# Float64 weights to float32: the sign written over the low word in place, in a 16-bit operation

## The chip, the cores and the metric

The kernel runs on one core of one Trainium2 chip. The metric is the device time of one execution in microseconds (us). The kernel before takes 461.08 us, the median of 3 runs (460.72 to 461.09). A few tenths of a microsecond is therefore what one run differs from the next.

## The reference

The reference is a recurrent attention (a gated outer-product state) followed by a multiplicative feed-forward block:

```python
f = 1 / (1 + exp(-f_logit))                       # B=4, H=8, S=768, D=48
for t in range(S):
    state = f[:, :, t, :, None] * state + einsum('bhd,bhe->bhde', k[:, :, t], v[:, :, t])
    y[:, :, t] = einsum('bhd,bhde->bhe', q[:, :, t], state)
x = y.transpose(0, 2, 1, 3).reshape(3072, 384)
a, b = x @ w1, x @ w2                             # 384 -> 1024
out = ((a * b) @ w3) @ w_out                      # 1024 -> 1024 -> 384
```

q, k, v and f_logit are float32. The four weight matrices are **float64**, because they are drawn as such and never cast. The chip's engines here work in float32, so the kernel reads every weight as a pair of 32-bit words and makes a float32 from them itself. That conversion is what the change touches.

## The kernel before, in words

**Stages.** The sequence is cut into 24 chunks of 128 positions (`NU`), which the kernel calls u = 0 to 23. For each chunk VectorE makes two scans of the gates (L529, L551) and scales q and k with them (L545 gives Q, L559 gives K), TensorE makes the pair products and the values (L582, L656, L675, L689, and L596 turns K), ScalarE copies, GpSimd masks (L712). Four chunks make a block of 512 tokens, and there are six blocks for the feed-forward part. Block 0 uses plain products (`up`, which calls the helper of L901), the later ones use schemes with fewer multiplications (L997, L1152). w3 and w_out are multiplied with each other once on the chip, in eight "folds" of eight matrix products (L1470), so that the block's second and third product become one.

**The conversion** is `fetch`. A piece of a weight matrix is loaded by DMA into a staging area of the tile `place` as pairs of 32-bit words, low word first. Four operations then make float32 of it:

1. `rest` on ScalarE (L1406) reads the low word as an integer and writes the float 2 + low * 2^-51 over it, so the low word's bits are 0x40000000 plus a small rounding carry. In its upper half there is always 0x4000.
2. `shifted` on VectorE (L1421) writes the high word, shifted left by 3, into the scratch `magnitudes`.
3. `signed` on VectorE (L1425) takes the sign bit of the high word, ors it with the low word from step 1, and writes the result to the destination (`dst()`).
4. `joined` on VectorE (L1431) adds the scratch to the destination as 32-bit integers. In the profile this integer addition is a custom operation that reads and writes 16-bit halves, so 1024 words are 2048 elements.

There are 16 pieces: A, C, B and D (the halves of w1 and w2, 1536 words per partition each), four of w_out (768 words) and eight of w3 (1024 words). A piece of w_out or w3 goes into one of three staging places, in turn, so that a load must wait until the piece that was there is no longer read. `got` names the operation after which the place is free.

**What sets the order.** The program is written as tasks with an engine, a cost, dependencies and a priority (`Plan`). A list scheduler plays them through with those costs and writes each engine's instructions in the order it found. Each engine then works strictly in this order and waits on semaphores. Where the scheduler finds TensorE without work in the first 130 us (`FULL`), it puts in idle matrix products on a constant tile (L402) to fill the gap:

```python
if t["eng"] == "PE" and t["at"] < FULL:
    n = int((t["at"] - ready_at) / 0.43)
    if ready_at and n:
        idle(n)
```

So a change of one cost can move instructions of every engine, and can put in or leave out idle products. In the trace one matrix product of float32 is two instructions.

Of the kernel before, what the change touches and what calls it, by code (L numbers as in the profile page):

```python
# [37 lines left out]
I32 = mybir.dt.int32  # L38
U32 = mybir.dt.uint32
U16 = mybir.dt.uint16  # L40
ALU = mybir.AluOpType
# [254 lines left out]
def ranged(ctx, tc, q, k, f_logit, v, w1, w2, w3, w_out, out, ident, w12, wc, left):  # L296

    nc = tc.nc
# [38 lines left out]
    def at(a, *shape):  # L337
        n = 1
        for m in shape:
            n *= m  # L340
        t = place[:, a : a + n]
        return t.rearrange("p (a b) -> p a b", a=shape[0]) if len(shape) == 2 else t
# [26 lines left out]
    plan = Plan()  # L369
# [97 lines left out]
    def moves(n, size, rate, emit, deps, prio, late=0.0, since=0.0, lanes=("lane",)):  # L467


        for j in range(n):  # L470
            i = plan.add("SP", 0.45, (lambda: None) if j else emit, [d] if j else deps, prio - j * 1e-3, takes=lanes, lag=0.85, since=since)
            d = i
            t = plan.add("DMA", size / n / rate, lambda: None, [i], prio - j * 1e-3, lag=1.1 + late, frees=[i])
        return t
# [905 lines left out]
    def holders(where, n):  # L1380

        return [g for a, m, gs in users if a < where + n and where < a + m for g in gs]

    def fetch(loads_, where, prio, due, dst, waits=(), deps=()):

        total = sum(n for _, n, _ in loads_)
        if not wide:
            def plain():
                d = dst()
                for at_, n, src in loads_:  # L1390
                    nc.sync.dma_start(d[:, at_ : at_ + n].rearrange("p (a m) -> p a m", a=src.shape[1]), src)
            return [plan.add("SP", 1.9 * total / 512, plain, list(waits), prio, lag=2.0)]
        raw = at(where, 2 * total).bitcast(U32)
        pairs_ = raw.rearrange("p (n two) -> p n two", two=2)
        lo, hi = pairs_[:, :, 0], pairs_[:, :, 1]
        held = holders(where, 2 * total)
        got = []
        users.append((where, 2 * total, got))
        landed, low = [], []
        for i, (at_, n, src) in enumerate(loads_):  # L1400
            def load(at_=at_, n=n, src=src):
                nc.sync.dma_start(raw[:, 2 * at_ : 2 * (at_ + n)].rearrange("p (a m) -> p a m", a=src.shape[1]), src.bitcast(U32))

            def rest(at_=at_, n=n):
                part_ = lo[:, at_ : at_ + n]
                nc.scalar.activation(part_.bitcast(F32), part_, AF.Copy, bias=2.0, scale=2.0**-51)  # L1406

            landed.append(moves(1, n, 400, load, held + list(deps), prio + 0.02 * i, SURE, lanes=("lane", "heavy")))
            asked.append(landed[-1])
            low.append(plan.add("ACT", 0.2 + 0.43 * n / 512, rest, [landed[-1]], due + 0.02 * i))  # L1410
        w = total / 512
        a0 = spot[0] if total <= 512 else (spot[0] + 512) // 1024 * 1024 % 2048
        if a0 + total > 2048:
            a0 = 0
        spot[0] = (a0 + (total + 511) // 512 * 512) % 2048
        m = magnitudes[:, a0 : a0 + total]
        mine = range(a0 // 512, (a0 + total + 511) // 512)
        s = {}

        def shifted():  # L1420
            nc.vector.tensor_scalar(m.bitcast(U32), hi, 3, None, ALU.logical_shift_left)  # L1421

        def signed():
            s["to"] = dst()
            nc.vector.scalar_tensor_tensor(  # L1425
                s["to"].bitcast(U32), hi, 0x80000000, lo, ALU.bitwise_and, ALU.bitwise_or
            )

        def joined():
            to = s["to"].bitcast(I32)  # L1430
            nc.vector.tensor_tensor(to, m.bitcast(I32), to, ALU.add)  # L1431

        past = [joins[i] for i in mine if i in joins]
        h = plan.add("DVE", 0.16 + 0.27 * w, shifted, landed + past, due, shared=True)
        g = plan.add("DVE", 0.16 + 0.53 * w, signed, [*low, h] + list(waits), due)
        j = plan.add("DVE", 0.16 + 0.53 * w, joined, [h, g], due - 1, shared=True)
        parts.append((g, j))
        joins.update({i: j for i in mine})
        got.append(g)
        return [j]  # L1440

    def weights():
        due = dict(zip(((0, 0), (1, 0), (0, 1), (1, 1)), DUE))
        for item in (x for x in EARLY if x in "ABCD"):
            half, which = divmod("ABCD".index(item), 2)
            w = (w1, w2)[which]
            cols = slice(half * KH * P, (half + 1) * KH * P)
            pieces[which, half] = fetch(
                [(kc * KH * P, KH * P, w[kc * P : kc * P + P, cols].unsqueeze(1)) for kc in range(KM)],
                EARLY_AT[item], turn_of(item), due[which, half],  # L1450
                lambda which=which, half=half: w12[:, which, half].rearrange("p k c -> p (k c)"),
            )

    def folding():
        done = []
        for i in range(0, KF, 2):
            src = w_out[i * P : (i + 2) * P].rearrange("(kc p) c -> p kc c", p=P)
            done += fetch(
                [(0, 2 * DM, src)], 2048 * ((13 + i // 2) % NRAW), 25 + 2.2 * i, 45 + 2.2 * i,
                lambda i=i: wos[:, i : i + 2].rearrange("p a c -> p (a c)"),  # L1460
                holders(10240, KF * DM) + [tk[3][nm] for nm in "qvs"], [tk[3]["z"]] if BEHIND and i < BEHIND else [],
            )
# [23 lines left out]
        for jc in range(KF):  # L1486
            src = w3[jc].unsqueeze(1)
            got = fetch(
                [(0, KF * P, src)], 2048 * ((17 + jc) % NRAW), 36 + 6 * jc, 50 + 6 * jc, w3_piece(jc),
                fp[jc - 2 : jc - 1] if jc >= 2 else holders(8192, 2048),  # L1490
            )
            fp.append(plan.add("PE", 5.15, fold(jc), got + done + fp[-1:], 0, takes=["f"]))
            folds.append(plan.add("ACT", 0.48, folded(jc), fp[-1:], -10, frees=fp[-1:]))
# [139 lines left out]
    for t in plan.order():  # L1633
        if t["eng"] == "PE" and t["at"] < FULL:
            n = int((t["at"] - ready_at) / 0.43)
# [382 lines left out]
```

## Time and profile before

| what | value |
|---|---|
| median of the runs | 461.08 us |
| span of the profiled execution, first to last instruction (the page gives no other time of it) | 459.2 us |
| TensorE busy (matrix products) | 450.8 us, 98% |
| VectorE busy | 370.7 us, 81% |
| ScalarE busy | 211.7 us, 46% |
| GpSimd busy | 66.3 us, 14% |
| conversion on VectorE: L1421, L1425, L1431, 16 each | 11.5, 20.5 and 20.9 us |
| conversion on ScalarE: L1406, 24 | 21.2 us |
| granted TensorE clock | 1.00 throughout |

The runs' median lies 1.9 us above the span of the profiled execution. A line of a timeline reads: start, duration, engine, source line, operation, output from inputs, shapes, how many; what follows in brackets is the time that the engine sat idle before it, and what ended that. A line of a group reads: busy time in all, mean ns of one, then the idle time before them with its releasers. "PE" is TensorE, "DVE" VectorE, "ACT" ScalarE, "POOL" GpSimd, "SPq" the queue of SyncE, which issues the DMAs.

### The profile page before, as it was taken

Reading aid. Unit: us, or ns where it says so; the run is one execution under the profiler, and the core shown is the slowest. Engines: PE = TensorE matmul, PEld = TensorE weight load, DVE = VectorE, ACT = ScalarE, POOL = GpSimd, SP = SyncE. Lnnn points to the kernel's source line nnn. Section 1 sums busy time; section 2 is a strip of 40 time slices with the busy share of each in tenths; the row PEclk is TensorE's granted clock in tenths of the full one; section 3 lists DMA queues with packets and bytes.
Section 4 is the critical chain, followed back from the end, with each engine's and each line's share of the span. In section 5 each row is a group of like instructions: output and inputs, shape, how many; then the busy total and the mean of one; then the engine's idle time right before and its main releaser. Section 6 shows DMA issues by size and latency. Waiting matters only on the chain.

```text
span 459.2 us, 11789 instructions
## 1 busy us (share of the span) xinstructions
PE 450.8 (98%) x4792; PEld 394.6 (86%) x4792; DVE 370.7 (81%) x651; ACT 211.7 (46%) x473; POOL 66.3 (14%) x90
## 2 busy tenths in 40 slices
PE   7999999999999999999999999999999999999996
PEld 6788886666899888889999888899899988889996
DVE  8997899999898999989999699896659466767641
ACT  3565344332233453543322256665665666665300
POOL 9331000121222531132222000000000000000000
PEclk9999999999999999999999999999999999999999
DMA  6997898833236664356322602436365522333111
GB/s 180 283 314 239 299 334 299 264 110 104 71 90 196 198 192 128 105 158 177 98 76 63 164 0 93 137 119 211 132 199 177 192 72 93 92 93 91 36 68 40
DMA packets 43309, 68.75 MB, mean 150 GB/s; under 512 B 5217, under 2 KB 28386, under 8 KB 42226
## 3 DMA queue, kind: packets, MB, share of 16 engines
q1 hardware_dynamic: 43250, 67.95, 48.2%
q8 instruction: 39, 0.64, 0.6%
q14 instruction: 20, 0.16, 0.1%
HBM read 58.88 MB, written 9.04 MB: 148 GB/s over the span
## 4 chain that ended last, share of the span: by engine, by line
PE 95%; DVE 1%; SPq 1%; DMA 1%; issue 0%; POOL 0%; POOLq 0%; DVEq 0%
PE f L901 24%; PE l L1152 15%; PE f L997 13%; PE f L1152 12%; PE f L1470 9%; PE l L901 9%; PE py L656 3%; PE pa L582 2%; PE pa L689 2%; PE f L596 2%; PE py L675 2%; PE f L402 1%; SPq L495 1%; DMA ab<-in_k_dram 1%; DVE K L559 0%
## 5 line engine op out<-in xcount | busy, mean ns | idle before, releaser
L712 POOL TENSOR_SCALAR_AFFINE_SELECT A<-A 64x512 f32<-64x512 f32 (+1 forms) x46 | 43.9, 955 | 110.5 <-ACT A L706 108.3
L1470 PE MATMUL f<-place 128*128 128x384 f32 x128 | 42.4, 487 | 0.0
L901 PE MATMUL f<-xt,w 128*128 128x256 f32 x192 | 42.1, 380 | 0.0
L901 PEld LDWEIGHTS f<-xt,w 128*128 128x128 f32 x192 | 36.3, 190 | 5.0
L1470 PEld LDWEIGHTS f<-place 128*128 128x128 f32 x128 | 23.9, 190 | 15.5
L901 PE MATMUL f<-place 128*128 128x192 f32 x176 | 31.9, 327 | 0.0
L997 PE MATMUL f<-xt,w 128*128 128x256 f32 x120 | 31.3, 380 | 0.0
L529 DVE TENSOR_TENSOR_SCAN fwd<-gate,floor 112x512 f32<-112x512 f32 x24 | 30.0, 1251 | 1.3 <-ACT gate L521 0.3
L551 DVE TENSOR_TENSOR_SCAN bwd<-gate,back 112x512 f32<-112x512 f32 x24 | 30.4, 1267 | 0.7
L901 PEld LDWEIGHTS f<-place 128*128 128x128 f32 x176 | 28.9, 190 | 0.4 <-issue 0.2
L848 ACT ACTIVATE ys<-py 112x512 f32<-112x512 f32 x22 | 13.1, 596 | 33.3 <-PE py L675 31.5
L997 PEld LDWEIGHTS f<-xt,w 128*128 128x128 f32 x120 | 22.5, 190 | 2.9
L901 PE MATMUL f<-wc,ab 128*128 128x192 f32 x128 | 23.6, 328 | 0.0
L1406 ACT ACTIVATE place<-place 128x512 f32<-128x512 uint32 (+2 forms) x24 | 21.2, 885 | 4.6 <-DMA place<-in_w_dram 4.0
L812 POOL TENSOR_TENSOR G<-lasts,gate 112x4 f32<-112x4 f32 x20 | 11.7, 586 | 75.1 <-ACT lasts L534 30.4
L901 PEld LDWEIGHTS f<-wc,ab 128*128 128x128 f32 x128 | 21.2, 190 | 0.3
L521 ACT ACTIVATE gate<-f 112x512 f32<-112x512 f32 x22 | 13.9, 632 | 16.0 <-DMA f<-in_f_logit_dram 7.0
L901 PE MATMUL l<-place 128*128 128x192 f32 x112 | 19.8, 326 | 0.0
L656 PEld LDWEIGHTS py<-A,vt 64*64 64x64 f32 (+1 forms) x672 | 13.3, 127 | 7.3 <-issue 6.5
L997 PE MATMUL f<-place 128*128 128x256 f32 x72 | 19.1, 386 | 0.0
L901 PEld LDWEIGHTS l<-place 128*128 128x128 f32 x112 | 18.5, 190 | 0.1
L656 PE MATMUL py<-A,vt 64*64 64x64 f32 (+1 forms) x672 | 18.0, 223 | 0.2
(288 smaller groups left out, 1066.7 us busy)
## 6 DMA issues: line engine op xcount, KB each, us to landing
place<-in_w_dram SPq DMA_DIRECT2D x21, 512.0 KB, 5.4
A<-in_w_dram SPq DMA_DIRECT2D x19, 512.0 KB, 4.0
place<-in_w_dram SPq DMA_DIRECT2D x8, 1024.0 KB, 6.2
q<-in_q_dram SPq DMA_DIRECT2D x46, 96.0 KB, 2.7
vt<-in_v_dram SPq DMA_DIRECT2D x23, 192.0 KB, 3.2
out_dram<-o SPq DMA_DIRECT2D x23, 192.0 KB, 2.9
k<-in_k_dram SPq DMA_DIRECT2D x44, 96.0 KB, 2.4
yt<-ys SPq DMA_DIRECT2D x44, 96.0 KB, 2.7
```

The source lines that it names most:

```text
L521: nc.scalar.activation(gate[u % 2][:, 0:NQ], fu, AF.Sigmoid)
L529: nc.vector.tensor_tensor_scan(s["P"], gate[u % 2][:, 0:NQ], floor, 0.0, ALU.mult, ALU.max)
L551: nc.vector.tensor_tensor_scan(s["R"][:, ::-1], gate[u % 2][:, NQ:0:-1], back[:, ::-1], 0.0, ALU.mult, ALU.max)
L656: done = nc.tensor.matmul(y_block(u, hp, par, half)[p0 : p0 + w], lhsT=s["v"][half * W : half * W + W, h * D : h * D + w], rhs=s["A"][half ...
L712: nc.gpsimd.affine_select(out=a, in_=a, pattern=pattern, compare_op=ALU.is_ge, fill=0.0, base=0, channel_multiplier=-1,)
L812: nc.gpsimd.tensor_tensor(s["G"], lasts[:, u], heads(gate[(u + 1) % 2][:, 0:NQ])[:, :, 0], ALU.mult)
L848: nc.scalar.activation(ys, py, AF.Copy, accum_out=ysum[:, u : u + 1])
L901: nc.tensor.matmul(out_, lhsT=lhs[i], rhs=rhs[i], start=start and i == 0, stop=i == len(lhs) - 1, skip_group_check=True,)
L997: nc.tensor.matmul(q[nm][:, which * TH : which * TH + TH], lhsT=lhs[i](which), rhs=rhs[i], start=start and which == 0 and i == 0, stop=i = ...
L1152: nc.tensor.matmul(banks[g, c][:, which * TH : which * TH + TH], lhsT=lhs, rhs=x_node(a), start=first and which == 0, stop=True, skip_grou ...
L1406: nc.scalar.activation(part_.bitcast(F32), part_, AF.Copy, bias=2.0, scale=2.0**-51)
L1470: nc.tensor.matmul(w3s["p", jc], lhsT=w3s[jc][:, kc * P : kc * P + P], rhs=wos[:, kc], start=(kc == 0), stop=(kc == KF - 1),)
```

## The change

`signed` no longer writes the destination. It works on 16-bit halves in the staging area: it reads the upper half of the high word, keeps the sign bit, ors 0x4000 to it and writes this over the upper half of the low word, which held 0x4000. It has one source instead of two. `joined` then reads the low word where it lies, in the staging area with a step of 8 bytes, adds the scratch, and writes the destination. Three things go with it: the planner's cost for `signed` is 0.16 + 0.27 us per 512 words in place of 0.16 + 0.53; the wait for a free destination moves from `signed` to `joined`; and the staging place is free after `joined` and not after `signed`.

```diff
+        halves_ = raw.bitcast(U16).rearrange("p (n four) -> p n four", four=4)
...
         def signed():
-            s["to"] = dst()
-            nc.vector.scalar_tensor_tensor(
-                s["to"].bitcast(U32), hi, 0x80000000, lo, ALU.bitwise_and, ALU.bitwise_or
-            )
+            nc.vector.tensor_scalar(halves_[:, :, 1], halves_[:, :, 3], 0x8000, 0x4000, ALU.bitwise_and, ALU.bitwise_or)
 
         def joined():
-            to = s["to"].bitcast(I32)
-            nc.vector.tensor_tensor(to, m.bitcast(I32), to, ALU.add)
+            nc.vector.tensor_tensor(dst().bitcast(I32), m.bitcast(I32), lo.bitcast(I32), ALU.add)
...
-        g = plan.add("DVE", 0.16 + 0.53 * w, signed, [*low, h] + list(waits), due)
-        j = plan.add("DVE", 0.16 + 0.53 * w, joined, [h, g], due - 1, shared=True)
+        g = plan.add("DVE", 0.16 + 0.27 * w, signed, [*low, h], due)
+        j = plan.add("DVE", 0.16 + 0.53 * w, joined, [h, g] + list(waits), due - 1, shared=True)
...
-        got.append(g)
+        got.append(j)
```

The lines of the three operations are L1421, L1425 and L1431 before, and L1422, L1425 and L1428 in the changed kernel.

The scheduler writes other orders from the new costs and dependencies. TensorE, where the first feed-forward product of block 0 begins (L901; L689 are the last products of the attention's chunk before it), before:

```order
L689 MATMUL pa<-place,kt 48x48
L402 MATMUL f_507<-floor 128x256 x2
L901 MATMUL f_510<-xt,w_59 128x256 x3
L901 MATMUL f_521<-xt,w_59 128x256 x3
L901 MATMUL f_530<-xt,w_59 128x256 x3
L656 MATMUL py<-A,place 64x64 x2
```

and in the changed kernel:

```order
L689 MATMUL pa<-place,kt 48x48
L901 MATMUL f_505<-xt,w_59 128x256 x3
L901 MATMUL f_515<-xt,w_59 128x256 x3
L901 MATMUL f_525<-xt,w_59 128x256 x3
L656 MATMUL py<-A,place 64x64 x2
```

One batch of idle products is gone. The other batches of L402 stay; the last of them comes further down the order.

VectorE, from the piece D of w2 to the second piece of w_out (shapes of 1536 are D, of 768 w_out; L943 ends a product of block 0), before:

```order
L1431 ISA w_59<-place,w_59 128x3072
L943 TENSOR_TENSOR ab<-f_642,ab 128x256
L529 SCALAR_TENSOR_TENSOR fwd<-gate_95,floor 112x512
L943 TENSOR_TENSOR ab<-f_653,ab 128x256
L1421 TENSOR_SCALAR place<-place 128x768
L1425 SCALAR_TENSOR_TENSOR place<-place 128x768
L1421 TENSOR_SCALAR place<-place 128x768
L943 TENSOR_TENSOR ab<-f_669,ab 128x256
L1425 SCALAR_TENSOR_TENSOR place<-place 128x768
L1431 ISA place<-place 128x1536
```

and in the changed kernel:

```order
L1428 ISA w_59<-place 128x3072
L943 TENSOR_TENSOR ab<-f_638,ab 128x256
L1422 TENSOR_SCALAR place<-place 128x768
L529 SCALAR_TENSOR_TENSOR fwd<-gate_95,floor 112x512
L943 TENSOR_TENSOR ab<-f_648,ab 128x256
L1425 TENSOR_SCALAR place<-place 128x768
L1428 ISA place<-place 128x1536
L943 TENSOR_TENSOR ab<-f_664,ab 128x256
L539 RECIPROCAL back<-fwd 112x4
L551 SCALAR_TENSOR_TENSOR bwd<-gate_95,back 112x512
L1422 TENSOR_SCALAR place<-place 128x768
L943 TENSOR_TENSOR ab<-f_680,ab 128x256
```

The backward scan of chunk 4 (L539, L551) now comes between the first two pieces of w_out; before, it came after all four of them and after two pieces of w3. Its product K (L559) follows it there, and on TensorE the turn of that K (L596) comes ahead of the first fold instead of behind the second.

SyncE, around the load of the fourth piece of w_out (128x2x768; the loads of 128x2048 are w3, L1402 before is L1403 in the changed kernel), before:

```order
L1402 DMA place<-in_w_dram 128x2048
L495 DMA f_103<-in_f_logit_dram 48x512 x2
L1402 DMA place<-in_w_out_dram 128x2x768
L495 DMA k_101<-in_k_dram 48x512 x2
L495 DMA q_99<-in_q_dram 48x512 x2
L1402 DMA place<-in_w_dram 128x2048 x3
```

and in the changed kernel:

```order
L1403 DMA place<-in_w_dram 128x2048
L495 DMA f_103<-in_f_logit_dram 48x512 x2
L495 DMA k_101<-in_k_dram 48x512 x2
L495 DMA q_99<-in_q_dram 48x512 x2
L1403 DMA place<-in_w_out_dram 128x2x768
L1403 DMA place<-in_w_dram 128x2048 x3
```

The load of the fourth piece of w_out now stands behind four loads of chunk 5's k and q.

## The prediction

> **What bounds the kernel now.** I read first the page's busy times and its chain of work that ended last, then the waits of TensorE alone.
>
> ```profile
> PE 450.8 (98%) x4792; PEld 394.6 (86%) x4792; DVE 370.7 (81%) x651; ACT 211.7 (46%) x473; POOL 66.3 (14%) x90
> PE 95%; DVE 1%; SPq 1%; DMA 1%; issue 0%; POOL 0%; POOLq 0%; DVEq 0%
> PE f L402 <- DVE floor L425: 1.7, 1, 1.7
> PE py L596 <- DVE K L559: 0.7, 1, 0.7
> PE pa L689 <- issue: 0.6, 1, 0.6
> PE f L596 <- DVE K L559: 0.4, 1, 0.4
> ```
>
> TensorE is busy for 450.8 of 459.2 us and 95% of the chain is on it. Its waits add up to 3.4 us, and none of them is at a product of the feed-forward part or at a fold (L901, L997, L1152, L1470). So a microsecond less of VectorE work is worth nothing by itself. The time moves only if TensorE gets something out of its way, or has to wait anew. One thing that is in its way isn't counted as a wait: the idle products of L402. Second view, TensorE in order of time where the feed-forward part begins, with the two operations on VectorE that it needs there:
>
> ```profile
> 28.61 0.27 PE L689 MATMUL pa<-place,kt 64*48 64x48 f32 x3
> 29.47 0.67 PE L689 MATMUL pa<-place,kt 64*48 64x48 f32 x29 [0.59 <-issue]
> 30.06 1.13 PE L402 MATMUL f<-floor 112*128 112x256 f32 x4
> 31.03 4.05 PE L901 MATMUL f<-xt,w 128*128 128x256 f32 x18
> 36.39 32.64 PE L901 MATMUL f<-xt,w 128*128 128x256 f32 x150
> 25.91 1.75 DVE L1425 SCALAR_TENSOR_TENSOR w<-place 128x1536 uint32<-128x1536 uint32 x1
> 27.69 1.76 DVE L1431 CUSTOM_DVE_ANT_0 w<-place,w 128x3072 uint16<-128x3072 uint16 x1
> 33.31 2.09 DVE L1431 CUSTOM_DVE_ANT_0 w<-place,w 128x3072 uint16<-128x3072 uint16 x1
> ```
>
> From 30.06 to 31.03 TensorE multiplies a constant. The piece that it needs, A, was ready at 27.69 + 1.76 = 29.45, so here the idle products themselves hold up the work, by 0.97 us. Third view, the busy time of the engines while the weights are converted and folded:
>
> ```profile
> 30.00:50.00 20.00, 19.90 (x154) 17.17 (x151) 15.98 (x17) 9.17 (x21) 4.03 (x3) 1.00 0.86 280
> 50.00:70.00 20.00, 20.00 (x93) 17.33 (x92) 18.03 (x29) 9.05 (x15) 0.20 (x1) 1.00 0.91 315
> 70.00:90.00 20.00, 20.00 (x129) 12.20 (x129) 18.34 (x24) 8.88 (x14) 1.96 (x2) 1.00 0.85 274
> 90.00:110.00 20.00, 20.00 (x296) 13.19 (x295) 19.05 (x25) 7.19 (x16) 4.59 (x6) 1.00 0.45 130
> ```
>
> The columns after the stretch's length are PE, PEld, DVE, ACT and POOL. VectorE has 4.02 + 1.97 = 5.99 us idle between 30 and 70, and 1.66 + 0.95 = 2.61 between 70 and 110. It is nearly as full as TensorE, and that idle time is all that it could take on without TensorE noticing.
>
> **The change part by part.** The prices come from the groups of the three operations, by shape:
>
> ```profile
> L1421 DVE TENSOR_SCALAR place<-place 128x1024 uint32<-128x1024 uint32 x8 | 5.5, 704 | 0.0
> L1421 DVE TENSOR_SCALAR place<-place 128x1536 uint32<-128x1536 uint32 x4 | 3.8, 958 | 1.7 <-DMA k<-in_k_dram 1.2 <-DMA place<-in_w_dram 0.4
> L1421 DVE TENSOR_SCALAR place<-place 128x768 uint32<-128x768 uint32 x4 | 2.2, 551 | 0.0
> L1425 DVE SCALAR_TENSOR_TENSOR place<-place 128x1024 uint32<-128x1024 uint32 x8 | 9.7, 1216 | 1.9 <-PE f L1470 1.5 <-ACT place L1406 0.4
> L1425 DVE SCALAR_TENSOR_TENSOR w<-place 128x1536 uint32<-128x1536 uint32 x4 | 7.0, 1753 | 1.6 <-ACT place L1406 1.6
> L1425 DVE SCALAR_TENSOR_TENSOR place<-place 128x768 uint32<-128x768 uint32 x4 | 3.8, 951 | 0.0
> L1431 DVE CUSTOM_DVE_ANT_0 place<-place 128x2048 uint16<-128x2048 uint16 x8 | 9.8, 1222 | 0.2
> L1431 DVE CUSTOM_DVE_ANT_0 w<-place,w 128x3072 uint16<-128x3072 uint16 x4 | 7.3, 1837 | 0.1
> L1431 DVE CUSTOM_DVE_ANT_0 place<-place 128x1536 uint16<-128x1536 uint16 x4 | 3.8, 950 | 0.0
> L1406 ACT ACTIVATE place<-place 128x1024 f32<-128x1024 uint32 x8 | 9.3, 1162 | 4.0 <-DMA place<-in_w_dram 4.0
> ```
>
> The sign operation: with one source it is of the kind of L1421, which reads every second word too and takes (958 - 704) / 512 = 0.50 ns per word. With two sources L1425 takes (1216 - 951) / 256 = 1.035 ns. No row shows an operation on VectorE that writes 2 of every 8 bytes. The nearest is ScalarE's L1406, which writes 4 of every 8 and takes 1162 ns for 1024. So the lower end is L1421's price, and the upper end today's price, with which nothing would be won; a higher one has no row behind it. I take L1421's, since source, step and engine are its own. That saves 8 x 512 + 4 x 795 + 4 x 400 = 4.1 + 3.2 + 1.6 = 8.9 us of VectorE: 3.2 + 1.6 + 2 x 0.51 = 5.8 before 70 us (A to D, w_out, two pieces of w3) and 6 x 0.51 = 3.1 after.
>
> The addition now reads one source with a step of 8 bytes. L1425 reads both of its sources so, and its 1216 ns equal the 1222 of the addition with everything side by side. That is the lower end: no price. The upper end is that it no longer takes two halves in the time of one word, 1.035 ns more per word. There are 17,408 words, so between 0 and 18.0 us. I take 0, nearest to L1425.
>
> [...]
>
> What moves: the idle batch of 0.97 us in front of L901 is gone. Nothing else holds L901 then: A would be ready at 25.91 + 0.96 + 1.76 = 28.6, before TensorE is free at 30.06, and so it would be at 29.45 with the sign operation at today's price; only the addition's upper end, 1.59 more for its 1536 words, would make it late. The next piece, C, was ready at 33.31 + 2.09 = 35.40 for products that begin after 36.39; both move up by about the same. On VectorE the backward scan and K of chunk 4 come ahead of most of the w_out pieces: 0.18 + 1.26 + 0.69, about 2.1 us by the rows below. Against the 5.8 us saved before 70 us this is covered; without that saving only the 5.99 us of idle time cover it. TensorE's turn of K, 0.55 us, comes ahead of the first fold and is missing after the second: no cost in sum.
>
> ```profile
> L539 DVE RECIPROCAL back<-fwd 112x4 f32<-112x4 f32 x24 | 4.3, 177 | 0.4
> L551 DVE TENSOR_TENSOR_SCAN bwd<-gate,back 112x512 f32<-112x512 f32 x24 | 30.4, 1267 | 0.7
> 72.55 0.69 DVE L559 TENSOR_TENSOR K<-k,bwd 112x512 f32<-112x512 f32 x1
> 79.19 0.55 PE L596 MATMUL f<-ident,K 112*128 112x112 f32 x4
> 61.84 0.98 ACT L1406 ACTIVATE place<-place 128x768 f32<-128x768 uint32 x1 [0.63 <-DMA place<-in_w_out_dram]
> 64.57 0.55 DVE L1421 TENSOR_SCALAR place<-place 128x768 uint32<-128x768 uint32 x1
> 66.89 0.95 DVE L1431 CUSTOM_DVE_ANT_0 place<-place 128x1536 uint16<-128x1536 uint16 x1
> 68.87 10.48 PE L1470 MATMUL f<-place 128*128 128x384 f32 x32
> 56.32 0.93 SPq L495 DMA_DIRECT2D q<-in_q_dram  x2
> 69.73 0.35 SPq L1402 DMA_DIRECT2D place<-in_w_dram  x1
> ```
>
> The waits: the staging place is free one addition later, but the sign operation ends 0.5 earlier: the next load of w3 (69.73, right when a sign operation ended) comes 1.22 - 0.51 = 0.7 us later at most. Behind it in SyncE's queue stand chunk loads. The last work in front of the first fold is the fourth w_out piece, ready at 66.89 + 0.95 = 67.84 for a fold at 68.87: 1.03 us to spare, the narrowest place that I found. There the change takes 0.97 and the turn gives 0.55 back.
>
> The sum: 459.2 - 0.97 = 458.2 us of span. The median of the runs lies 1.9 above the span; 461.08 - 0.97 = **460.1 us**. Neither a slower nor a faster VectorE enters it, as long as it stays under the bounds above.
>
> **The rivals.**
>
> First, the wait moves to the first fold. The load of the fourth w_out piece now stands behind four more loads, 2 x 0.93 = 1.9 us of SyncE's time. If its addition came 1.9 later, at 69.7, the fold (due at 68.87 - 0.97 + 0.55 = 68.45) would wait 1.25 us: the gain and 0.3 more are gone, 461.08 - 0.97 + 1.25 = 461.4. Against it: the data had landed at 61.84 and VectorE began with it only at 64.57, so the queue has 2.7 us to lose. Chance 0.17.
>
> Second, stepping by 8 bytes costs the addition, and VectorE becomes the bound (the other side). The place is the conversions of w_out and w3, the price p per word. Before 70 us: 11,264 words (A to D, w_out, two pieces of w3), less the 5.8 saved, plus 2.1 moved in, and 0 to 5.99 us of idle time takes it up. After 70: 6,144 words, less 3.1, with 0 to 2.61 idle. At the upper end, p = 1.035, that is a wait of 2.0 to 8.0 and 0.6 to 3.3, in the middle 6.9: 467.0. At half of it, p = 0.52, it is 0 to 2.2 and 0 to 0.1, in the middle 1.1: 461.2. So about 464, the middle of the two. It decides from p = 0.33 on, where 11,264 p exceeds 3.7: an addition of 1024 words at 1.56 us in place of 1.22. L1425's price speaks against it; that no row has this form speaks for it. Chance 0.16. [...]
>
> Third, the sign operation gets no faster because of its narrow writes (the change does not do what it says). Then the 2.1 us moved ahead of the w_out pieces meet 0 to 5.99 of idle time: a wait of 0 to 2.1, in the middle 1.05, 461.2. Chance 0.12.
>
> Fourth, more is won. The wait of 0.59 at L689, which no engine explains, could vanish with another order: 459.5. Chance 0.07.
>
> **How the numbers follow.** The forecast has the remaining 0.48; its own range is 459.6 to 460.6, the half batch on either side. The range goes up to 464.0, over the first and third rival and the lower half of the second, and down to 459.2. A measurement tells a change from none at about 0.2%, 0.92 us. The forecast lies at 0.97, so I count 0.30 of its 0.48 as faster and 0.18 as the same; with the 0.07, faster 0.37. Same: 0.18, 0.12 of the first rival and 0.06 of the third, 0.36. Slower: the second rival's 0.16 and 0.11 of the others, 0.27.
>
> **What would show it.** The sign operation at about 704, 958 and 551 ns, and the addition at 1222 for 1024 words. No L402 between L689 and L901, and L901 at 30.1. No wait of TensorE at L1470, and its last product 1 us earlier. The prediction is wrong if TensorE's waits name L1470 with VectorE, if VectorE's idle time between 50 and 110 us is gone, or if the addition is above 1.6 us.

## The result, and the profile after

The changed kernel takes **465.6 us**, the median of 5 runs (462.58 to 468.54), beside 461.08 (460.72 to 461.17) of the kernel before: a ratio of 1.0103, 95% interval 1.0067 to 1.0138. It is slower; 460.1 was predicted, and 465.6 lies above the range. Its runs also scatter over 6 us, those of the kernel before over half a microsecond here, and over 1.6 to 3.7 us in the larger groups of runs below: more than the few tenths that the first three runs of it let one expect. The profiled execution is the one of 468.54; its span is 466.8 us, 7.6 more than before.

First the page of the changed kernel, busy time and the chain that ended last, and then its groups of the conversion by shape (L1425 is the sign operation, L1428 the addition):

```profile
PE 451.6 (97%) x4788; PEld 394.1 (84%) x4788; DVE 373.0 (80%) x651; ACT 211.9 (45%) x473; POOL 71.9 (15%) x90
PE 71%; DVE 12%; DMA 9%; POOL 3%; issue 2%; SPq 2%; ACT 1%; DVEq 0%; POOLq 0%; ACTq 0%
L1425 DVE TENSOR_SCALAR place<-place 128x1024 uint16<-128x1024 uint16 x8 | 10.5, 1317 | 3.7 <-ACT place L1407 3.7
L1425 DVE TENSOR_SCALAR place<-place 128x1536 uint16<-128x1536 uint16 x4 | 7.6, 1900 | 0.9 <-ACT place L1407 0.9
L1425 DVE TENSOR_SCALAR place<-place 128x768 uint16<-128x768 uint16 x4 | 4.1, 1033 | 0.0
L1428 DVE CUSTOM_DVE_ANT_0 place<-place 128x2048 uint16<-128x2048 uint16 x8 | 9.8, 1220 | 0.0
```

TensorE has as much to do as before (451.6 us against 450.8), and 95% of the chain has become 71%. So the 7.6 us are nearly all waits. The addition costs what it did (1220 ns against 1222). The sign operation, with one source in place of two, is not faster but 8 to 9% slower: 1317, 1900 and 1033 ns against 1216, 1753 and 951. All 16 take 10.5 + 7.6 + 4.1 = 22.2 us, where the prediction counted on 11.6 and the kernel before needed 20.5.

The waits of TensorE, and the two stretches in which the weights are folded (the columns behind the stretch's length are PE, PEld, DVE, ACT, POOL, clock, DMA share):

```profile
PE f L1467 <- DVE place L1428: 3.8, 1, 3.8
PE f L596 <- DVE K L559: 2.0, 3, 1.1
PE f L402 <- DVE floor L425: 1.7, 1, 1.7
PE f L402 <- DVE ab L943: 1.6, 1, 1.6
PE f L901 <- DVE w L1428: 0.5, 1, 0.5
50.00:70.00 20.00, 20.00 (x95) 17.32 (x94) 19.67 (x32) 8.04 (x14) 0.53 (x1) 1.00 0.89 300
70.00:90.00 20.00, 16.18 (x113) 9.52 (x112) 16.88 (x22) 5.69 (x11) 1.96 (x2) 1.00 0.66 219
```

VectorE is full from 50 to 70 (19.67 of 20 us; 18.03 before). From 70 to 90 TensorE stands still for 3.8 us, and VectorE, too, is less busy than before (16.88 against 18.34): something that both need comes late. The timeline shows what, from the transfers of w3 to the third fold:

```profile
61.82 7.05 SPq L1403 DMA_DIRECT2D place<-in_w_dram  x3
68.92 0.89 SPq L495 DMA_DIRECT2D f<-in_f_logit_dram  x2
74.91 1.31 DVE L1425 TENSOR_SCALAR place<-place 128x1024 uint16<-128x1024 uint16 x1 [0.40 <-ACT place L1407]
78.31 0.63 ACT L521 ACTIVATE gate<-f 112x512 f32<-112x512 f32 x1 [3.36 <-DMA f<-in_f_logit_dram]
79.21 1.14 ACT L1407 ACTIVATE place<-place 128x1024 f32<-128x1024 uint32 x1
80.38 1.30 DVE L1425 TENSOR_SCALAR place<-place 128x1024 uint16<-128x1024 uint16 x1 [2.08 <-ACT place L1407]
83.04 1.21 DVE L1428 CUSTOM_DVE_ANT_0 place<-place 128x2048 uint16<-128x2048 uint16 x1
84.40 5.40 PE L1467 MATMUL f<-place 128*128 128x384 f32 x16 [3.82 <-DVE place L1428]
```

SyncE issues the w3 loads one by one as additions set staging places free; the third of the row above, which loads the fourth w3 piece, goes out at 68.54, right after an addition of a w_out piece, and is issued by 68.87. Behind it in the queue stands the load of the gates for the next chunk: issued at 68.92, landed only at 78.2. ScalarE waits for it at L521, and behind L521 in ScalarE's order stands the low part of that fourth piece (79.21), whose data are there by 77.61, when VectorE shifts its high words. VectorE's sign operation of it follows at 80.38, and behind it in VectorE's order, at 83.04, the third addition of a w3 piece, which releases the third fold. The third sign operation had ended at 74.91 + 1.31 = 76.22. So, with additions and folds taken in the order in which the trace has them, the third fold stands behind work on a piece that it doesn't need yet. A lateness on VectorE has gone around through SyncE, a transfer and ScalarE, and has grown on the way, most of it in the transfer: in e6 below, which has the same order, the gates' load is issued 1.0 us earlier (67.88), but L521 runs 4.7 us earlier (73.58). Why the transfer takes so much longer here, no run separates.

### The profile page after: what moved, and what is told of

Read it like the earlier page. It is cut to its first block, busy times and chain, and to the rows that moved or that the text cites. A ratio compares the mean times of both kernels' runs of the same rounds, so it can differ in the third digit from the quotient of the medians.

```text
span 466.8 us, 11791 instructions
## 1 busy us (share of the span) xinstructions
PE 451.6 (97%) x4788; PEld 394.1 (84%) x4788; DVE 373.0 (80%) x651; ACT 211.9 (45%) x473; POOL 71.9 (15%) x90
## 4 chain that ended last, share of the span: by engine, by line
PE 71%; DVE 12%; DMA 9%; POOL 3%; issue 2%; SPq 2%; ACT 1%; DVEq 0%; POOLq 0%; ACTq 0%
PE f L901 18%; PE l L1152 15%; PE f L1152 11%; PE f L997 10%; PE l L901 6%; DMA f<-in_f_logit_dram 5%; PE py L656 2%; PE l L997 2%; DMA place<-in_w_dram 2%; DVE place L1425 2%; DVE place L1428 2%; DVE place L1500 2%; PE py L675 1%; PE pa L582 1%; PE pa L689 1%
## 5 line engine op out<-in xcount | busy, mean ns | idle before, releaser
L712 POOL TENSOR_SCALAR_AFFINE_SELECT A<-A 64x512 f32<-64x512 f32 (+1 forms) x46 | 49.6, 1079 | 104.1 <-ACT A L706 102.0
L901 PE MATMUL f<-xt,w 128*128 128x256 f32 x192 | 42.6, 381 | 0.5 <-DVE w L1428 0.5
L901 PEld LDWEIGHTS f<-xt,w 128*128 128x128 f32 x192 | 36.1, 190 | 5.5 <-issue 0.6
L901 PE MATMUL f<-place 128*128 128x192 f32 x224 | 40.4, 327 | 0.0
L1467 PEld LDWEIGHTS f<-place 128*128 128x128 f32 x128 | 23.8, 190 | 19.4 <-ACT wc L1474 4.4
L901 PEld LDWEIGHTS f<-place 128*128 128x128 f32 x224 | 36.7, 190 | 0.1
L529 DVE TENSOR_TENSOR_SCAN fwd<-gate,floor 112x512 f32<-112x512 f32 x24 | 31.3, 1303 | 1.6 <-ACT gate L521 0.4
L551 DVE TENSOR_TENSOR_SCAN bwd<-gate,back 112x512 f32<-112x512 f32 x24 | 30.2, 1260 | 0.8
L521 ACT ACTIVATE gate<-f 112x512 f32<-112x512 f32 x22 | 13.9, 631 | 30.2 <-DVE bwd L551 15.7
L1425 DVE TENSOR_SCALAR place<-place 128x1024 uint16<-128x1024 uint16 (+2 forms) x16 | 22.3, 1392 | 4.7 <-ACT place L1407 4.7
L997 PE MATMUL f<-xt,w 128*128 128x256 f32 x100 | 25.7, 379 | 0.0
L901 PE MATMUL f<-wc,ab 128*128 128x192 f32 x128 | 23.6, 328 | 0.0
L812 POOL TENSOR_TENSOR G<-lasts,gate 112x4 f32<-112x4 f32 x20 | 11.6, 579 | 70.3 <-ACT gate L521 19.6
L901 PEld LDWEIGHTS f<-wc,ab 128*128 128x128 f32 x128 | 21.2, 190 | 0.4
L997 PEld LDWEIGHTS f<-xt,w 128*128 128x128 f32 x100 | 18.9, 190 | 2.5
L1543 ACT ACTIVATE A<-A,back 128x512 f32<-128x512 f32 x23 | 17.9, 778 | 0.2
L1268 DVE TENSOR_TENSOR place<-ab 128x512 f32<-128x512 f32 x24 | 16.4, 684 | 1.0 <-PE f L901 1.0
```

The costliest lines, as they stand in the source:

```text
L529: nc.vector.tensor_tensor_scan(s["P"], gate[u % 2][:, 0:NQ], floor, 0.0, ALU.mult, ALU.max)
L551: nc.vector.tensor_tensor_scan(s["R"][:, ::-1], gate[u % 2][:, NQ:0:-1], back[:, ::-1], 0.0, ALU.mult, ALU.max)
L712: nc.gpsimd.affine_select(out=a, in_=a, pattern=pattern, compare_op=ALU.is_ge, fill=0.0, base=0, channel_multiplier=-1,)
L901: nc.tensor.matmul(out_, lhsT=lhs[i], rhs=rhs[i], start=start and i == 0, stop=i == len(lhs) - 1, skip_group_check=True,)
L997: nc.tensor.matmul(q[nm][:, which * TH : which * TH + TH], lhsT=lhs[i](which), rhs=rhs[i], start=start and which == 0 and i == 0, stop=i = ...
L1268: nc.vector.tensor_tensor(abs_[j], x, y, op)
```

## The experiments

Three theories were set against each other. **A**: the planner was told 0.27 us per 512 words for an operation that takes 0.585, so it wrote an order that cannot be kept. **B**: the staging place is free only after the addition, so loads come later. **C**: the longer operation itself costs the time. The kernel before ran again beside each group of runs; its medians there are 460.90 (e1 to e4), 460.70 (e5 to e7), 460.71 (e8 to e10) and 461.06 (e11, e12).

### e1: the changed kernel, planned with the true price

```diff
-        g = plan.add("DVE", 0.16 + 0.27 * w, signed, [*low, h], due)
+        g = plan.add("DVE", 0.15 + 0.585 * w, signed, [*low, h], due)
```

> The changed kernel with one number altered: the planner is told that the sign operation takes 0.15 us and 0.585 us per 512 words (what the trace of the changed kernel shows: 1317 ns for 1024 words, 1900 for 1536) in place of 0.16 and 0.27, which was off by 0.6 to 0.9 us for each of the 16. Same operations, same waits; only the order is planned anew. Three theories stand against each other. A, the loss comes from an order planned with a price that is too low: 460.5 to 462, and the wait of 3.8 us of TensorE at the third fold goes. B, it comes from the staging place that is released only by the addition: the price changes nothing of that, 463 to 467. C, it is the longer operation itself, 16 of them together some 1.7 us longer than in the kernel before: 462 to 463, spread over many short waits.

Measured: 461.71 us (461.37 to 462.17, 12 runs), ratio 1.0021 (1.0013 to 1.003). The operation is as long as in the changed kernel, and TensorE waits for no fold and nowhere for a weight longer than 0.2 us:

```profile
L1425 DVE TENSOR_SCALAR place<-place 128x1024 uint16<-128x1024 uint16 x8 | 10.5, 1318 | 0.0
PE l L1152 <- DVE place L1119: 1.3, 1, 1.3
PE f L901 <- DVE w L1428: 0.2, 1, 0.2
```

Of the 4.5 us over the kernel before, one cost in the planner leaves 0.8, and it takes the scatter away. That is A. B does not explain the loss, since the place is released as late as in the changed kernel. The 0.8 that is left has a place in the trace: a wait for VectorE at a product of a later block, at 267.75 us, that the kernel before doesn't have.

### e2, e3, e4: price and release apart, with the old operation

```diff
 e2 (kernel before)
-        g = plan.add("DVE", 0.16 + 0.53 * w, signed, [*low, h] + list(waits), due)
+        g = plan.add("DVE", 0.16 + 0.27 * w, signed, [*low, h] + list(waits), due)
 e3 (kernel before)
-        got.append(g)
+        got.append(j)
 e4: both
```

> The kernel before, operations and waits as they were, only the planner is told the changed kernel's price for the sign operation (0.27 us per 512 words in place of 0.53; it really takes 1216 ns for 1024 words). A (false price): slower by 1 to 4 us, 462 to 465, with a wait of TensorE at a fold or at an up-projection behind VectorE. B (later release) and C (the operation): no part of either is in it, 460.5 to 461.8.

> The kernel before, only the staging place is given free after the addition instead of after the sign operation. The price stands at its true 0.53. B (later release): the loads of w_out and w3 go out later by about the addition's 1.22 us and what VectorE does between, the ring of transfers runs later in 50 to 90 us, 462.5 to 465. A and C: nothing of theirs is in it, 460.5 to 461.8.

> The kernel before with both: the low price and the later release, but with the two-source sign operation of 1216 ns per 1024 words. It has nearly the changed kernel's plan without its operation. A and B together, without C: 463 to 466, as slow as the changed kernel, with the wait at the third fold. C alone: 460.5 to 461.8, since the operation is the old one. If it lies between, near 463.5, the rest of the changed kernel's loss, about 1.7 us, belongs to the operation.

Measured: e2 463.60 us (463.25 to 464.41), ratio 1.0062 (1.0048 to 1.0076); e3 460.81 (460.40 to 461.44), ratio 1.0000 (0.9991 to 1.0008); e4 463.16 (461.79 to 466.66), ratio 1.0047 (1.0029 to 1.0065).

So a false price alone, with no operation of the conversion changed, makes the kernel before 2.7 us slower. The later release alone costs nothing in sum. It does write another order, though: e3's profile has e1's wait of 1.3 us at L1152 (266.78) and, against that, one batch of idle products less, about 1 us. Nor can a cost be seen on top of the false price: the intervals of e2 and e4 overlap. But e4 scatters over 4.9 us and e2 over 1.2, and in e4's profile, of its slowest execution, TensorE waits 1.06 us at the third fold, which it doesn't in e2's. B falls as a cause of the loss by itself; that it has a part in where a wait falls is not excluded.

Of e2, TensorE's waits:

```profile
PE f L596 <- DVE K L559: 1.6, 2, 1.2
PE f L402 <- DVE ab L943: 1.6, 1, 1.6
122.45 0.60 PE L596 MATMUL f<-ident,K 112*128 112x112 f32 x4 [1.19 <-DVE K L559]
132.00 1.13 PE L402 MATMUL f<-floor 112*128 112x256 f32 x4 [1.57 <-DVE ab L943]
```

The two longest new ones lie at 122 and 132 us, well after the conversions. A reading that fits is that VectorE carries its arrears along until TensorE reaches products that need its last results. Not all of the wait at 132 is arrears: a wait of 0.6 us at the same place stands in e6 and e8 too (0.59 and 0.58), where the price is true. Against the plan each sign operation in e2 is late by 0.52, 0.78 or 0.39 us (1216 - 700 for 1024 words, where 700 is 0.16 + 2 x 0.27; so for 1536 and 768): 8 x 0.52 + 4 x 0.78 + 4 x 0.39 = 8.8 us in all. In the changed kernel it is 8 x 0.62 + 4 x 0.93 + 4 x 0.47 = 10.6 us. The remaining 2.4 us from e4 to the changed kernel go along with those further 1.7 us of the operation; that they come from them is not shown, since the two orders differ.

### e5 and e10: the operation by itself

> Not the computation (the output is zeros): 16 forms of one VectorE operation, each six times on 128x1024, to price the sign operation by itself. It was 1317 ns for 1024 words in the changed kernel, where the one-source shift took 690 and the two-source operations 1216 to 1222. Causes that could make it so long: the narrow destination (2 bytes written in every 8), then 16-bit to a contiguous 16-bit or 32-bit destination is near 690 and contiguous 16-bit to every fourth half near 1300; the narrow source, the other way round; the 16-bit type itself, then contiguous to contiguous is at 1300 as well; two operations in one instruction instead of one, then the form with one operation is near 690; source and destination in one tile, then writing to another tile is near 690. On whole 32-bit words with a step of 8 bytes: near 690 if only the half word is dear, near 1300 if any stepped destination is.

The groups of e5, 1024 elements each (`raw` is read and written with a step of 8 bytes; `hflat` is contiguous 16-bit words; `flat` contiguous 32-bit words, of whose upper halves L62 and L64 write, 4 bytes apart):

```profile
L58 DVE TENSOR_SCALAR raw<-raw 128x1024 uint16<-128x1024 uint16 x6 | 8.0, 1341 | 0.0
L60 DVE TENSOR_SCALAR raw<-raw 128x1024 uint16<-128x1024 uint16 x6 | 8.0, 1341 | 0.0
L56 DVE TENSOR_SCALAR raw<-raw 128x1024 uint16<-128x1024 uint16 x6 | 7.7, 1289 | 0.0
L68 DVE TENSOR_SCALAR raw<-hflat 128x1024 uint16<-128x1024 uint16 x6 | 7.6, 1274 | 0.0
L62 DVE TENSOR_SCALAR flat<-raw 128x1024 uint16<-128x1024 uint16 x6 | 4.4, 741 | 0.0
L66 DVE TENSOR_SCALAR hflat<-raw 128x1024 uint16<-128x1024 uint16 x6 | 4.0, 674 | 0.0
L70 DVE TENSOR_SCALAR hflat<-hflat 128x1024 uint16<-128x1024 uint16 x6 | 2.5, 413 | 0.0
L72 DVE TENSOR_SCALAR raw<-raw 128x1024 uint32<-128x1024 uint32 x6 | 4.1, 675 | 0.0
```

L56 is the changed kernel's sign operation. It is neither its source (L66 reads the same halves and takes 674), nor its two operations in one instruction (L60 has one), nor working within one tile (L58 writes another). L68 has a contiguous source and still takes 1274: the destination alone makes the price, 16-bit words written 8 bytes apart. Whole 32-bit words to the same places cost 675 (L72).

> Not the computation (the output is zeros): the destination's width and step alone, 512 elements in 128 partitions, six times each, the source always contiguous. 16-bit words written every 2, 4, 8 and 16 bytes, 32-bit words every 4, 8 and 16 bytes on VectorE, and the same idea on ScalarE (32-bit words every 4 and 8 bytes, 16-bit every 4 and 8). If a 16-bit word costs more because of its distance from the next one (an area of 8 bytes is touched for 2), then 16-bit at 16 bytes is dearer again than at 8, and 32-bit words at 16 bytes dearer than at 8. If it is the half word with a gap of more than one word, 16-bit at 8 and 16 bytes are alike, at about twice the price at 4 bytes, and 32-bit words are alike at every step. ScalarE: no price for steps with 32-bit words (1158 ns against 1162 for 1024 in the two kernels), open for 16-bit words.

The groups of e10, 512 elements with contiguous sources: 16-bit words every 2, 4, 8 and 16 bytes (L62, L64, L66, L68), 32-bit words every 4, 8 and 16 (L70, L72, L74), and ScalarE writing 16-bit words every 4 and 8 bytes (L80, L82):

```profile
L62 DVE TENSOR_SCALAR hflat<-hflat 128x512 uint16<-128x512 uint16 x6 | 1.7, 285 | 0.0
L64 DVE TENSOR_SCALAR raw<-hflat 128x512 uint16<-128x512 uint16 x6 | 2.7, 456 | 0.9 <-DMA raw<-in_w_dram 0.8
L66 DVE TENSOR_SCALAR raw<-hflat 128x512 uint16<-128x512 uint16 x6 | 4.4, 732 | 0.2
L68 DVE TENSOR_SCALAR raw<-hflat 128x512 uint16<-128x512 uint16 x6 | 7.8, 1299 | 0.2
L70 DVE TENSOR_SCALAR flat<-raw 128x512 uint32<-128x512 uint32 x6 | 2.5, 419 | 1.3 <-DMA raw<-in_w_dram 1.3
L72 DVE TENSOR_SCALAR raw<-raw 128x512 uint32<-128x512 uint32 x6 | 2.6, 428 | 0.2
L74 DVE TENSOR_SCALAR raw<-raw 128x512 uint32<-128x512 uint32 x6 | 3.7, 621 | 0.2
L80 ACT CAST raw<-flat 128x512 bf16<-128x512 f32 x6 | 4.6, 759 | 0.2
L82 ACT CAST raw<-flat 128x512 bf16<-128x512 f32 x6 | 8.0, 1325 | 0.2
```

With 16-bit words the time goes up with the distance, without a ceiling up to 16 bytes; ScalarE shows the same from 4 to 8 bytes. With 32-bit words a step of 8 bytes costs 428 - 419 = 9 ns more than one of 4, and 16 bytes 621 - 428 = 193 ns more than 8.

### e6 and e9: the operation made short, in both orders

The sign is written as a whole 32-bit word. In e6 all else is the changed kernel's, in e9 that of e1, to the last instruction of every engine.

```diff
-            nc.vector.tensor_scalar(halves_[:, :, 1], halves_[:, :, 3], 0x8000, 0x4000, ALU.bitwise_and, ALU.bitwise_or)
+            nc.vector.tensor_scalar(lo, hi, 0x80000000, 0x40000000, ALU.bitwise_and, ALU.bitwise_or)
```

> The changed kernel with the sign written as whole 32-bit words over the low words (4 of every 8 bytes instead of 2), still one source and still priced at 0.27. It leaves out the low word's rounding carry, so the last bit of a converted weight can differ. If the half-word destination was what made the operation slow, it now takes near 704 ns for 1024 words, the planner's price is true, and the sum of the prediction applies: 460.1, within 459.6 to 460.6. If any stepped destination costs that much, it stays at 1.2 to 1.3 us and the time at 463 to 467.

> The changed kernel with whole 32-bit words (its carry of the low word is left out, as in the run with whole words before), but planned with 0.585 us per 512 words: it has the order and the waits of the run with the true price of the 16-bit operation (461.71), and only that operation is shorter, 690 ns for 1024 words in place of 1318. This takes the operation alone, in one order. If the length of the operation costs time by itself in this order, 460.0 to 461.0, that is 0.7 to 1.7 us less than 461.71; and as the plan was made for slow operations nothing waits for VectorE in 50 to 130 us and there is little scatter. If its length is hidden when the plan knows it: 461.4 to 462.0, no change.

| order planned with | sign operation of 1024 words | median (lowest to highest) |
|---|---|---|
| 0.27 per 512 words | 1317 ns (changed kernel) | 465.6 (462.58 to 468.54) |
| 0.27 | 690 ns (e6) | 460.81 (460.21 to 466.23) |
| 0.585 | 1318 ns (e1) | 461.71 (461.37 to 462.17) |
| 0.585 | that of e6, 690 ns there (e9) | 461.60 (461.18 to 466.10) |

The same 0.63 us per operation are worth 4.8 us in the first order and 0.1 in the second. Neither the price nor the length decides, but an operation that is longer than its plan; one that is shorter gains nothing in this order. So A, in this form, and C only within the order that A wrote. The changed kernel and e6 have the same order of instructions on TensorE in their traces, and so have e1 and e9.

e6 is also the case that the prediction assumed, an operation of 690 ns with a true price, and it shows how much of the gain was there. Its median lies just above the range of its expectation, and its ratio to the kernel before is 1.0019 (0.9996 to 1.0041): no gain. Of its profiled execution:

```profile
L1425 DVE TENSOR_SCALAR place<-place 128x1024 uint32<-128x1024 uint32 x8 | 5.5, 690 | 1.2 <-ACT place L1407 1.2
30.16 4.15 PE L901 MATMUL f<-xt,w 128*128 128x256 f32 x18
73.58 0.63 ACT L521 ACTIVATE gate<-f 112x512 f32<-112x512 f32 x1 [1.15 <-DMA f<-in_f_logit_dram]
129.49 1.13 PE L402 MATMUL f<-floor 112*128 112x256 f32 x4 [0.59 <-DVE ab L943]
```

L901 starts at 30.16, 0.87 us earlier than the 31.03 before; the gate that was at 78.31 in the changed kernel is at 73.58. But at 129.49 TensorE waits 0.59 us for VectorE where it did not wait before: 0.87 - 0.59 leaves 0.28, and the spans differ by 0.2 (459.0 and 459.2).

### e7 and e8: the sign at the destination

A version of its own: ScalarE writes the low part to the destination, the sign operation writes 16-bit words there, 4 bytes apart, and the place is released as early as before. e7 plans with 0.53, e8 with 0.30.

```diff
-                part_ = lo[:, at_ : at_ + n]
-                nc.scalar.activation(part_.bitcast(F32), part_, AF.Copy, bias=2.0, scale=2.0**-51)
+                if "to" not in s:
+                    s["to"] = dst()
+                nc.scalar.activation(s["to"][:, at_ : at_ + n], lo[:, at_ : at_ + n], AF.Copy, bias=2.0, scale=2.0**-51)
...
-            nc.vector.tensor_scalar(halves_[:, :, 1], halves_[:, :, 3], 0x8000, 0x4000, ALU.bitwise_and, ALU.bitwise_or)
+            up = s["to"].bitcast(U16).rearrange("p (n two) -> p n two", two=2)[:, :, 1]
+            nc.vector.tensor_scalar(up, halves_[:, :, 3], 0x8000, 0x4000, ALU.bitwise_and, ALU.bitwise_or)
```

> A version of its own: ScalarE writes the low part straight to the destination tile, without a step, the sign operation writes its 16 bits there (2 of every 4 bytes instead of 2 of every 8), the addition works in place in the destination as in the kernel before; the staging place is free after the sign operation and the shift, as before; the planner is told 0.53. If the price of the sign operation goes by the distance between the words written, it falls below 1317 ns for 1024 words and VectorE wins up to 0.5 us for each: 460 to 461. If it goes by the half word, it stays at 1.3 us: 461 to 462, no gain, with the waits for the w3 places now ahead of ScalarE, where 1 us more is the price of being wrong.

> The version that writes the low part and the sign at the destination, with the planner now told what its sign operation takes: 0.15 us and 0.30 us per 512 words (755 ns for 1024 words, 598 for 768, 1048 for 1536 in its trace) in place of 0.53. VectorE wins 0.46 us for each conversion of 1024 words against the kernel before, and the staging place is free as early as before. If a false price, in whichever direction, is what makes the times go up and scatter (the version with 0.53 had 460.8 to 465.6): 460.0 to 460.8, with little scatter. If the relief of VectorE is what lets the plan pull other work forward and run into new waits, it stays at 460.7 to 462.5 with scatter. If the new wait of ScalarE on the places of w3 is the cause, it also stays there, with TensorE or VectorE waiting for the low part in 70 to 110 us.

Measured: the operation takes 755 ns for 1024 words, as the distance of 4 bytes lets one expect from e5 (741 to 774). e7 462.42 us (460.83 to 465.64), ratio 1.0048 (1.0026 to 1.0069); e8 461.55 (460.46 to 462.70), ratio 1.0018 (1.0004 to 1.0033). VectorE is relieved of 0.46 us per conversion of 1024 words, and neither version is faster. e7 lies outside both ranges of its expectation: it is 1.7 us slower though its operation is shorter than its plan, and as only its fastest execution (460.83) was profiled, the cause stays open. So an operation longer than its plan is one way to lose time here, and not shown to be the only one. e8 shows the middle case of its expectation: with a true price the scatter is smaller, but the new order has waits of its own (1.4 us ahead of L689 that no engine explains, 0.6 us each for `ab` at 130.22 and for a scan, L529, at 173.55). VectorE does wait for the low parts of w3 (3.3 us in all ahead of the eight in e7, 1.7 in e8), but TensorE nowhere waits between 60 and 130 us in e7, and not for a fold in e8.

### e11: the old order, the short operation

```diff
-            nc.vector.scalar_tensor_tensor(
-                s["to"].bitcast(U32), hi, 0x80000000, lo, ALU.bitwise_and, ALU.bitwise_or
-            )
+            nc.vector.tensor_scalar(
+                s["to"].bitcast(U32), hi, 0x80000000, 0x40000000, ALU.bitwise_and, ALU.bitwise_or
+            )
```

> The kernel before, in its own order to the last instruction of every engine, only the sign operation has one source: 690 ns for 1024 words in place of 1216. It leaves out the low part of the weights (they are cut off rather than rounded), and with it the wait of the sign operation for ScalarE. VectorE gets 8.9 us of relief of which nothing is planned into other work. If the relief is worth something to TensorE in the kernel before, it shows here: the wait of 0.59 us ahead of L689 and those of 0.7 and 0.4 us for L559 shrink, 459.4 to 460.3. If those waits have other causes (in the order there is nothing for TensorE to do while it waits, and the idle batch of 0.97 us stands where it stood), 460.5 to 461.0, no change: then what the prediction counted on could only come from a new order.

Measured: 460.79 us (459.99 to 461.56), ratio 0.999 (0.9977 to 1.0004): no change that can be measured. TensorE's waits in the kernel before were 1.7, 0.7, 0.6 and 0.4; here:

```profile
PE f L402 <- DVE floor L425: 1.7, 1, 1.7
PE pa L689 <- issue: 0.4, 1, 0.4
PE f L596 <- DVE K L559: 0.2, 1, 0.2
```

The sign operations take 11.5 us in place of 20.5. These 9.0 us less of VectorE take at most 1.1 us from the waits and nothing certain from the time. In each of the three orders in which it was tried (e6, e9, e11) a shorter conversion had next to nothing to give.

### e12: the changed kernel again

> The changed kernel once more, as it is, beside the same runs of the kernel before: its first profile was taken of its slowest execution (468.54 of 462.58 to 468.54). If the wait of 3.8 us at the third fold is what the order and the long operation bring each time, it stands in this profile too, with 2 us or more, and the time is 464 to 467. If it was this one execution's, TensorE's waits add up to 2 to 4 us elsewhere (L596 and L402 behind VectorE, 105 to 140 us) and the time is 462.5 to 465.7 all the same.

Measured: 466.71 us (465.41 to 470.60, 6 runs), ratio 1.0142 (1.011 to 1.0173). The wait at the third fold is there again, 2.1 us, and more than its own length is lost there. Of its profile, the third fold and the granted clock (the column behind POOL) just before it and in the 12 us that follow:

```profile
81.92 7.09 PE L1467 MATMUL f<-place 128*128 128x384 f32 x16 [2.05 <-DVE place L1428]
78.00:82.00 4.00, 1.95 (x7) 0.88 (x6) 3.83 (x6) 1.81 (x3) 1.98 (x2) 1.00 0.09 27
82.00:86.00 4.00, 4.00 (x8) 2.12 (x9) 3.96 (x6) 0.00 (x0) 0.00 (x0) 0.63 0.76 256
86.00:90.00 4.00, 4.00 (x16) 2.50 (x15) 3.57 (x4) 1.15 (x4) 0.00 (x0) 0.94 0.90 303
90.00:94.00 4.00, 4.00 (x14) 2.36 (x13) 3.45 (x6) 3.22 (x4) 0.66 (x1) 1.00 1.00 225
```

The fold took 7.09 us in place of 5.40: after the wait the granted clock was 0.63 from 82 to 86 us. So the fold ended 2.05 + 1.69 = 3.7 us later than without the wait and with the 5.40.

## Why the prediction was wrong, step by step

**What bounds the kernel: right.** TensorE does, and less VectorE work is worth nothing by itself (e11).

**The price of the sign operation: wrong, and the step from which the rest follows.** "So the lower end is L1421's price, and the upper end today's price", "a higher one has no row behind it", "I take L1421's, since source, step and engine are its own". The destination was not its own: 704 was taken, 1317 measured, above the upper end of 1216. Instead of a saving of 8.9 us on VectorE there was a loss of 22.2 - 20.5 = 1.7. That no row showed a write of 2 in every 8 bytes was said, and the bound was then taken from ScalarE's row, which writes whole 32-bit words; e5 shows that those cost VectorE no more at a step of 8 bytes (L72, 675 ns) than side by side (L78, 685 ns).

**The addition: right.** No price for its stepped source was taken; 1220 ns for 1024 words were measured against 1222. The second rival (about 464) came near the measured time for a reason that did not occur: no run shows its price of up to 1.035 ns more per word. By itself, too, the addition takes the same 1226 ns for 1024 words with its second source at a step of 8 bytes and with both sources side by side (L82 and L84 of e5).

**The idle batch and L901: right in kind, given back later.** The batch is gone in both profiles. With the short operation L901 came at 30.16 (30.1 predicted); with the real one at 30.52, as it waited 0.5 us for A, and at 29.80 without a wait in the second profile (e12). But "461.08 - 0.97 = 460.1" stops at 31 us. In e6 the 0.87 won there are followed by a new wait of 0.59 at 129.5. The working took it that time won once stays won, and looked for new waits between 30 and 110 us only.

**The third rival: the right case with the wrong price.** That the operation gets no faster was given 0.12 and 461.2. e4 is nearly that case (the old lengths, planned as if halved, the place released later), and it took 463.2; e2, without the release, 463.6. The rival weighed only the 2.1 us moved ahead against idle time and found a wait "of 0 to 2.1". The arrears are those of all 16 operations against their plan, 8.8 us, and the longest new waits of e2 stand where the weighing did not look, at 122 and 132 us.

**The release of the staging place: the estimate "0.7 us later at most" was too small.** Its reckoning rested on a sign operation that ends 0.5 us earlier. The third w3 load in a row was issued at 66.02 in the kernel before, when the sign operation of a w_out piece had ended (65.04 + 0.95). It is issued at 68.54 in the changed kernel, when that piece's addition has ended: 2.5 us later. Even with the short operation (e6) it is 1.5 later, at 67.50. The gates' load behind it makes the third fold late. That little depends on it for the time was right: the later release alone cost nothing in sum (e3), and the wait at the fold disappears with a true price (e1) or a short operation (e6).

**The first fold: right.** No wait is listed at it; it began at 68.83. The wait named as a sign of failure came at the third.

**The range** ended at 464.0. It took the operations' prices as its unknowns; that the order itself depends on a price, and that an operation longer than its price can become a wait anywhere in it, was not among them.

## What to carry to other kernels

Where a planner writes the order from costs, a new operation's cost has to be measured before it is planned with: 16 operations, each some 0.6 us longer than planned, cost 4.8 us here, while the same 0.6 us cost 0.1 where the plan knew of them. A duration may be borrowed from another row only if the destination's width and step agree too, not the source's alone: at a step of 8 bytes 1024 words of 32 bits took 690 ns here (e6), of 16 bits 1317. And if the bounding engine waits only 3.4 us in all, relief of another engine has these waits and the filler products in its order as its ceiling, and an early gain counts only when the engine's last wait of the stretch is earlier as well.

## What the runs showed of the hardware

- VectorE writes 16-bit words with a step at a price that grows with the distance: 285, 456, 732 and 1299 ns for 512 at 2, 4, 8 and 16 bytes; ScalarE took 759 at 4 and 1325 at 8. The 32-bit words took 419, 428 and 621 at 4, 8 and 16. So 32-bit words cost 1.02 times as much at 8 bytes as side by side, and 1.48 times at 16; 16-bit words cost at 8 bytes 2.6 times as much as side by side and 1.6 times as much as at 4 bytes.
- After a wait of TensorE of 2.05 us the granted clock was 0.63 in 82 to 86 us and 0.94 in 86 to 90 (e12), and the same was seen in e4, after 1.94 us at 133 us: 0.67 in 132 to 136 and 0.90 in 136 to 140. After the 3.82 us in the first profile of the changed kernel it stayed at 1.00 from 84 to 96. In e12 that is 4 x (0.37 + 0.06) = 1.72 us of full clock less, in e4 4 x (0.33 + 0.10) = 1.72 as well, estimates from the means of these windows; the fold of e12 took 1.69 us longer, so the two agree. What decides whether the clock is lower after a wait stays open: after the longest of the three it was not.
- It stays open what makes single executions of e6, e7 and e9 3 to 5 us longer than the medians of their runs (466.23, 465.64 and 466.10 us). Their mean clocks, 0.995, 0.994 and 0.992 against 0.998 to 1.000 in most others, point to the same loss of clock; none of them was profiled. It explains a part only: 1.72 us of clock less, as in e12 and e4, lower the mean over 464 us by 0.004, so an estimate is one such loss in each of the first two and two in the third, 1.7 to 3.4 us. The kernel before has two such executions as well, 463.37 and 463.78 us at 0.996.
